# Moving the preparation of the down weights one pass earlier in a linear-attention and gated-FFN kernel

## The chip, the cores and the metric

The kernel runs on one core of a Trainium2 chip. The metric is the device time of one execution in microseconds. The core has a matrix engine (TensorE, in the profile PE, with its weight loads as PEld), VectorE (DVE), ScalarE (ACT), GpSimd (POOL) and SyncE (SP), which here issues every DMA. Each engine works through its own instructions in program order and waits on semaphores for the others.

## The reference

```python
def _A_ref(x, wqkv, wo):                       # linear attention, 32 heads of 32
    qkv = reshape(x @ wqkv)
    phi = lambda t: where(t > 0, t + 1, exp(t)) + 1e-6
    pq, pk = phi(q), phi(k)
    kv = einsum("bhsd,bhse->bhde", pk, v);  z = einsum("bhsd->bhd", pk)
    o = einsum("bhqd,bhde->bhqe", pq, kv) / (einsum("bhqd,bhd->bhq", pq, z)[..., None] + 1e-6)
    return reshape(o) @ wo

def _B_ref(x, w_gate, w_up, w_down):           # gated FFN, no nonlinearity
    return ((x @ w_gate) * (x @ w_up)) @ w_down

x = x + _A_ref(_layernorm(x), A_wqkv, A_wo)
x = x + _B_ref(_layernorm(x), B_w_gate, B_w_up, B_w_down)
x = x + _A_ref(_layernorm(x), A_wqkv, A_wo)    # the same weights a second time
x = x + _B_ref(_layernorm(x), B_w_gate, B_w_up, B_w_down)
```

x has 2048 rows of 1024 in bfloat16, and the FFN is 3584 wide (`F`).

## The kernel before, in words

The rows x stay on chip in the tile `X`. Layer li = 0 and 2 is the attention (`layer_A`), li = 1 and 3 the FFN (`layer_B`). Work buffers come from three queues that are filled and emptied in program order: 16 `slots` of [128 x 4096] bfloat16, 13 `temps` of [128 x 512] float32 and the 8 PSUM `banks`. Whoever takes a buffer waits until its last user has left it. The order of instructions on every engine is the order in which the program writes them: plans of the form `at(step, f, args)` hang side work onto the steps of a matmul loop.

**Attention.** A first phase computes k and v and their sums. The query phase then runs 44 steps (`NQ + OLAG`). In step i it issues the denominator of item i - 4 (`den_step`, `LAG` 4: a matmul, two ACT functions, and L490, a product on DVE of two tiles in SBUF), the query product of item i (`q_step`, 8 matmuls, then in `phi` one ACT function and the DVE operations L193 and L194), and the output product of item i - 12 (`out_step`, 8 matmuls, L498, and the DVE addition L500 into `X`). An item is one of 8 column blocks of one of 4 row groups; the output product of a group needs all eight columns of it. `ahead_of` adds the layer norm and the transposes (through DMA) for the next FFN from step 18, the first two loads of FFN weights at 22 and 28, their casts on ACT from 25, and their sums on DVE at 35 and 41, with `t_sums`, sums of the rows, between.

**FFN.** `ffn_pass` is run four times (q = 0 to 3): two passes of 1024 rows in each of the two FFN layers. A pass has 14 `quad`s, each 256 columns of gate and of up. A quad computes its two products as seven block products instead of eight (Strassen's scheme in the form of Winograd): 14 groups of 4 matmuls (L622), whose partial sums ACT copies out (L627, L668) and DVE adds (L630) and multiplies (L633). Since block sums need a fixed scale, the weights are cast to float16 with a power of two that follows from their size, `scw`.

- In pass q = 0 each quad also casts the weights of quad j + 2 (`W.cast`, L294, four casts of 128x1024 on ACT), forms their sums (`W.sums`, L309, four on DVE) and writes both to a scratch in memory, `wcache` (`W.store`). The later passes read them from there.
- The down product of pass q = 0 is `down_plain`: four blocks of 28 x 4 matmuls (L778) with bfloat16 weights. Beside it, ACT squares the down weights (L746) to find their size, and `scale_begin(1)`, `scale_end(1)` turn this into a scale: a sum on DVE, a transpose on TensorE, a few small DVE operations.
- In pass q = 1 the quads 0, 1, 3, 4, 6, 7, 9 (`at_quad`) also prepare the down weights, four rows of blocks at a time: `prep_load`, `prep_cast` (L596, four casts of 128x1024), `prep_sums` (L605, four on DVE) and `prep_store` (four DMAs) into the scratch `dcache`.
- The down product of passes 1 to 3 is `down_seven`: seven block products of 14 x 4 matmuls (L875) that take raw pieces of the down weights, cast on the way (L582), and combined pieces from `dcache`.

In layer 0's first phase `scan` measures the gate and up weights, with squares on ACT (L201) and statistics on DVE (L206). The two lines that order the casts in a quad are

```python
if j + 2 < NQD: W.cast(j + 2, i)
if q == 1 and j in at_quad: prep_cast(at_quad[j], i)
```

and `cast(0)` stands before the copy of L668, `cast(1)` to `cast(3)` behind it.

Of the kernel before, what the change touches and what calls it, by code (L numbers as in the profile page):

```python
# [34 lines left out]
def kernel(  # L35
# [100 lines left out]
    wst = const.tile([P, 32, 6], F32, tag="wst", name="wst")  # L136
    dsq = const.tile([P, 32], F32, tag="dsq", name="dsq")
    bexp = const.tile([P, 3], F32, tag="bexp", name="bexp")
    scw = const.tile([P, 3], F32, tag="scw", name="scw")
    kap = const.tile([P, 2], F32, tag="kap", name="kap")  # L140
    wcache = [dram.tile([P, 2, 4096], F16, tag=f"wc{j}", name=f"wc{j}") for j in range(NQD)]
# [55 lines left out]
    def scan(i):  # L197
# [11 lines left out]
        return square, stats  # L209

    qsum = {}

    def norm_sums(m, q):
        if m == 0:
            nc.vector.tensor_reduce(out=q[:, 0:1], in_=wsq[:, 0:7], axis=AX.X, op=ALU.add)
            nc.vector.tensor_reduce(out=q[:, 1:2], in_=wsq[:, 7:10], axis=AX.X, op=ALU.add)
            mv = small.tile([P, 2], F32, tag="mv", name="mv")
            nc.vector.bn_aggr(out=mv[:], in_=wst[:])
            nc.vector.scalar_tensor_tensor(out=mv[:, 0:1], in0=mv[:, 0:1], scalar=mv[:, 0:1], in1=mv[:, 1:2],
                                           op0=ALU.mult, op1=ALU.add)  # L220
            nc.vector.scalar_tensor_tensor(out=q[:, 1:2], in0=mv[:, 0:1], scalar=float(32 * NB), in1=q[:, 1:2],
                                           op0=ALU.mult, op1=ALU.add)
        else:
            nc.vector.tensor_reduce(out=q[:, 0:1], in_=dsq[:], axis=AX.X, op=ALU.add)

# [13 lines left out]
    def scale_end(m):  # L239
# [17 lines left out]
        nc.vector.tensor_scalar(out=sc, in0=sc, scalar1=WS, scalar2=None, op0=ALU.mult)  # L257
        if m == 0:
            nc.vector.tensor_scalar(out=kap[:, 0:1], in0=bexp[:, 0:1], scalar1=bexp[:, 1:2],
                                    scalar2=(WS * XS) ** -2, op0=ALU.mult, op1=ALU.mult)  # L260
        else:
            nc.vector.tensor_scalar(out=kap[:, 1:2], in0=kap[:, 0:1], scalar1=bexp[:, 2:3],
                                    scalar2=1.0 / (WS * HS), op0=ALU.mult, op1=ALU.mult)

    class Weights:
        def __init__(self, cached):
            self.cached = cached
            self.wt = {}
            self.ws = {}
# [12 lines left out]
        def store(self, j):  # L282
            if not self.cached:
                nc.sync.dma_start(out=wcache[j][:, 0], in_=self.wt[j][:].bitcast(F16))
# [56 lines left out]
    def layer_A(li, ahead):  # L341
# [163 lines left out]

        LAG, OLAG = 4, 12
        NQ = NG * KD
        for i in range(NQ + OLAG):
# [16 lines left out]
            if li == 0 and i == 16:  # L525
                scale_end(0)
            for f, *args in ahead.get(i, []):
                f(*args)
# [12 lines left out]
    def ffn_pass(li, p, W):  # L541
# [8 lines left out]
        final = li == 3 and p == 1  # L550

        def load_wd(n, i):
            s = slots.get()
            nc.sync.dma_start(out=s[:, 0:WPC * NB].rearrange("p (k n) -> p k n", n=NB),
                              in_=wd_v[:, i * WPC:(i + 1) * WPC, n * NB:(n + 1) * NB])
            wd.append(s)

# [26 lines left out]

        def first_wd(i):
            if q == 0:
                load_wd(0, i)
            else:
                load_piece()

        at_quad = {0: 0, 1: 1, 3: 2, 4: 3, 6: 4, 7: 5, 9: 6}
# [21 lines left out]
        def quad(j):  # L613
            a, b, c = ([banks.get() for _ in range(2)] for _ in range(3))
            if j % 2 == 0:
                hs.append(slots.get())
            hv = (v3 if q == 0 else h3)(hs[j // 2], 2 * G)
            u1, u2, u3 = {}, {}, {}
# [13 lines left out]
            def mul(r, g, x, y):  # L632
                nc.vector.scalar_tensor_tensor(out=hv[:, 2 * (j % 2) + r, g * G:(g + 1) * G], in0=x[:],  # L633
                                               scalar=kap[:, 0:1] if q == 0 else HS, in1=y[:],
                                               op0=ALU.mult, op1=ALU.mult)

            def cast(i):
                if j + 2 < NQD:
                    W.cast(j + 2, i)
                if q == 1 and j in at_quad:  # L640
                    prep_cast(at_quad[j], i)
                if q > 0 and j == NQD - 1 and i < 2:
                    cast_piece(0, (i,))
# [44 lines left out]
        for j in range(NQD):  # L688
            if j + 2 < NQD:
                W.load(j + 2)  # L690
            elif j == NQD - 2:
                first_wd(0)
            else:
                first_wd(1)
                first_wd(2)
            if q == 1 and j - 1 in at_quad:
                prep_store(at_quad[j - 1])
            if q == 1 and j in load_at:
                prep_load(load_at[j])
            quad(j)  # L700
            if j + 2 < NQD:
                W.sums(j + 2)
            if q == 1 and j in at_quad:
                prep_sums(at_quad[j])
# [26 lines left out]
        nl = (li, 1) if p == 0 else (li + 1, 0)  # L731
        W2 = Weights(True)
        if q == 0:
            down_plain(li, p, hs, wd, load_wd, at, run, finish, xrow, nl, W2)
        else:
            down_seven(li, p, hs, wd, load_piece, cast_piece, ORDER, at, run, finish, xrow, nl, W2, load_a, final)
        return W2

    def down_plain(li, p, hs, wd, load_wd, at, run, finish, xrow, nl, W2):
        load_wd(0, 3)  # L740

        def square(i):
            for r in range(4):
                w = WPC * NB // 4
                t = temps.get()
                nc.scalar.activation(out=t[:].bitcast(BF16)[:, 0:w], in_=wd[i][:, r * w:(r + 1) * w],  # L746
                                     func=ACT.Square, accum_out=dsq[:, 4 * i + r:4 * i + r + 1])
                temps.put(t)

        for u in range(2 * TPG):  # L750
            t = nl[1] * 2 * TPG + u
            at(1 + 3 * u, ln_stats, nl[0], t)
            at(2 + 3 * u, ln_norm, nl[0], t)
            at(3 + 3 * u, tr_tile, nl[0], t)
        for i in range(3):
            at(6 + 7 * i, load_wd, 1, i)
        for i in range(4):
            at(3 + 7 * i, square, i)
        for i in range(4):
            at(KF + 24 + 5 * i, square, 4 + i)  # L760
        at(KF + 21, load_wd, 1, 3)
        for i in range(4):
            at(2 * KF + 10 + 5 * i, t_sums, li, 1, i)
        at(3 * KF + 8, W2.load, 0)
        at(3 * KF + 17, W2.load, 1)
        at(3 * KF + 21, prep_load, 0)
        at(3 * KF + 25, prep_load, 1)
        at(3 * KF, scale_begin, 1)
        at(3 * KF + 6, scale_end, 1)

        for blk in range(4):
            n, g = divmod(blk, 2)
            bs = [banks.get() for _ in range(TPG)]
            for f in range(KF):
                s = wd[n * NPC + f // WPC]
                for tl in range(TPG):
                    t0 = g * G + tl * P
                    nc.tensor.matmul(out=bs[tl][:], lhsT=v3(hs[f // 4], 2 * G)[:, f % 4, t0:t0 + P],  # L778
                                     rhs=s[:, (f % WPC) * NB:(f % WPC + 1) * NB],
                                     start=(f == 0), stop=(f == KF - 1), skip_group_check=True)  # L780
                if g == 1:
                    if f % WPC == WPC - 1:
                        slots.put(s)
                    if n == 1 and f % 4 == 3:
                        slots.put(hs[f // 4])
                run(blk * KF + f)
            for tl in range(TPG):
                _, o, _ = xrow(g, tl, n)
                nc.vector.tensor_tensor(out=o, in0=o, in1=bs[tl][:], op=ALU.add)
                banks.put(bs[tl])  # L790
                finish(g, tl, n)

    def down_seven(li, p, hs, wd, load_piece, cast_piece, ORDER, at, run, finish, xrow, nl, W2, load_a, final):
        sg = [slots.get(), slots.get()]
# [36 lines left out]
        if not final:  # L831
            if p == 0:
                for i in range(4):
                    at(60 + 4 * i, t_sums, li, 1, i)
                at(75, W2.load, 0)
                at(89, W2.load, 1)
            else:
# [8 lines left out]
        def read(o, g, tl, n, src, keep=None):  # L846
            _, x, _ = xrow(g, tl, n)
            nc.vector.scalar_tensor_tensor(out=o, in0=src, scalar=kap[:, 1:2], in1=x if keep is None else keep,
                                           op0=ALU.mult, op1=ALU.add)
# [51 lines left out]
    def ahead_of(li, W):  # L901
# [16 lines left out]
        at(41, W.sums, 1)  # L918
        at(42, W.store, 0)
        at(43, W.store, 1)  # L920
        return plan
# [6 lines left out]
    for li in (0, 2):  # L928
        W = Weights(li > 0)
        layer_A(li, ahead_of(li + 1, W))  # L930
# [31 lines left out]
```

## Time and profile before

| what | value |
|---|---|
| median of 3 runs | 1526.24 us (1525.51 to 1526.77) |
| the profiled execution, its own time | 1525.0 us |
| span of the profiled execution | 1523.2 us |
| DVE busy | 950.8 us (62%) |
| ACT busy | 678.6 us (45%) |
| DMA | 249.44 MB, mean 164 GB/s |

The span runs from the first to the last instruction in the trace; the time of the same execution is 1.8 us longer. A group in the profile reads: line, engine, operation, output <- inputs, sizes, count, busy microseconds, mean nanoseconds of one, idle time of the engine before it, and what ended that. Matmuls are pipelined: a busy share of TensorE near 100% says that it always had one in hand. In a timeline the bracket behind a line gives the engine's idle time before it and the releaser.

### The profile page before, as it was taken

To read this page: it belongs to the slowest core of one execution; us is meant where nothing else is said; L and a number is where in the kernel's file an instruction comes from. 1 tells how busy PE (TensorE), PEld (TensorE's weight loads), DVE (VectorE), ACT (ScalarE), POOL (GpSimd) and SP (SyncE) were. 2 spreads that over 40 slices of the span, in tenths; PEclk is the share of its full clock that TensorE was granted. 3 is DMA by queue.
4 is the path that set the end of the run, shared out by engine and by line. 5 is a ranking of instruction groups with operands and counts; after the bars stand their busy time and mean duration, and the time that the engine had idled before them with its cause. 6 is when DMAs were issued, how large, how long until landed. Compare 5 with 4: busy or idle time off the path is not lost.

```text
span 1523.2 us, 18375 instructions
## 1 busy us (share of the span) xinstructions
PE 1511.1 (99%) x7211; PEld 694.2 (46%) x7211; DVE 950.8 (62%) x1595; ACT 678.6 (45%) x1067; POOL 1.7 (0%) x18
## 2 busy tenths in 40 slices
PE   7999999999999999999999999999999999999999
PEld 3454444444444444444444444444444444444444
DVE  6567888777762376657355557865555864555552
ACT  4678665666562255532223355533334222333320
POOL 0000000000000000000000000000000000000000
PEclk9999999999999999999999999999999999999999
DMA  7693045888670776737513300464333578333523
GB/s 242 160 304 97 5 93 179 275 250 267 220 176 28 277 281 240 266 141 207 197 21 83 91 0 8 145 215 158 139 111 128 155 259 336 123 138 139 188 78 128
DMA packets 185287, 249.44 MB, mean 164 GB/s; under 512 B 68209, under 2 KB 162161, under 8 KB 170865
## 3 DMA queue, kind: packets, MB, share of 16 engines
q1 hardware_dynamic: 185200, 248.28, 50.6%
q8 instruction: 56, 0.92, 0.2%
q14 instruction: 31, 0.25, 0.1%
HBM read 191.63 MB, written 40.89 MB: 153 GB/s over the span
## 4 chain that ended last, share of the span: by engine, by line
PE 96%; DVE 2%; ACT 1%; DMA 0%; issue 0%; ACTq 0%
PE b L622 44%; PE b L875 17%; PE b L351 12%; PE b L469 7%; PE b L498 7%; PE b L778 6%; PE b L483 1%; PE b L368 1%; ACT s L201 1%; DVE wst L206 1%; PE b L451 0%; DVE st L157 0%; DVE s L194 0%; DVE f L193 0%; DMA X<-in_A_x_dram 0%; DVE xn L169 0%
## 5 line engine op out<-in xcount | busy, mean ns | idle before, releaser
L622 PE MATMUL b<-s,s 128*128 128x512 f16 x3136 | 677.5, 379 | 0.0
L622 PEld LDWEIGHTS <-s 128*128 128x128 f16 x3136 | 306.8, 98 | 370.0
L627 ACT COPY f<-b 128x512 f32<-128x512 f32 x336 | 196.9, 586 | 409.4 <-PE b L622 409.4
L630 DVE TENSOR_TENSOR f<-f,b 128x512 f32<-128x512 f32 x336 | 229.8, 685 | 237.2 <-ACT f L627 223.2
L875 PE MATMUL b<-s,s 128*128 128x512 f16 x1176 | 254.3, 379 | 0.0
L351 PE MATMUL b<-s,s 128*128 128x512 bf16 x1024 | 224.5, 381 | 2.1 <-DMA s<-in_A_wqkv_dram 1.8
L875 PEld LDWEIGHTS <-s 128*128 128x128 f16 x1176 | 115.1, 98 | 138.7
L351 PEld LDWEIGHTS <-s 128*128 128x128 bf16 x1024 | 100.2, 98 | 122.1 <-issue 2.8
L192 ACT ACTIVATE f<-b 128x512 f32<-128x512 f32 x128 | 75.7, 596 | 109.8 <-PE b L351 85.6
L469 PE MATMUL b<-s,s 128*128 128x512 bf16 x512 | 120.3, 379 | 0.0
L498 PE MATMUL b<-s,s 128*128 128x512 bf16 x512 | 118.5, 379 | 0.0
L582 ACT ACTIVATE s<-s,scw 128x1792 f16<-128x1792 bf16 x36 | 62.3, 1782 | 80.9 <-DMA s<-in_B_w_down_dram 80.9
L778 PE MATMUL b<-s,s 128*128 128x512 bf16 x448 | 96.9, 379 | 0.0
L193 DVE TENSOR_SCALAR f<-f 128x512 f32<-128x512 f32 x128 | 53.8, 420 | 68.5 <-ACT f L192 67.9
L633 DVE SCALAR_TENSOR_TENSOR s<-f,f 128x512 f16<-128x512 f32 x126 | 87.2, 692 | 8.4 <-DMA dc<-s 4.1
L157 DVE BATCH_NORM_STATS2 st<-X 128x6 f32<-128x512 bf16 x128 | 81.8, 681 | 3.6 <-DMA X<-in_A_x_dram 3.6
L498 PEld LDWEIGHTS <-s 128*128 128x128 bf16 x512 | 50.0, 98 | 60.6 <-DVE s L490 0.4
L469 PEld LDWEIGHTS <-s 128*128 128x128 bf16 x512 | 50.0, 98 | 59.7 <-issue 0.3
L778 PEld LDWEIGHTS <-s 128*128 128x128 bf16 x448 | 43.8, 98 | 52.7
L485 ACT ACTIVATE f<-b,eps 128x512 f32<-128x512 f32 x64 | 44.2, 691 | 45.4 <-PE b L483 45.4
L169 DVE TENSOR_SCALAR xn<-X,mv,rstd 128x1024 bf16<-128x1024 bf16 (+1 forms) x64 | 34.8, 544 | 47.2 <-ACT rstd L167 46.7
L294 ACT ACTIVATE s<-s,scw 128x1024 f16<-128x1024 bf16 x56 | 61.4, 1142 | 0.9 <-DMA s<-in_B_w_gate_dram 0.9
(81 smaller groups left out, 852.8 us busy)
## 6 DMA issues: line engine op xcount, KB each, us to landing
s<-wc SPq DMA_DIRECT2D x84, 1024.0 KB, 6.5
wc<-s SPq DMA_DIRECT2D x28, 1024.0 KB, 5.1
s<-in_B_w_down_dram SPq DMA_DIRECT2D x26, 896.0 KB, 5.1
s<-dc SPq DMA_DIRECT2D x24, 896.0 KB, 5.8
s<-in_A_wqkv_dram SPq DMA_DIRECT2D x12, 1024.0 KB, 7.7
s<-in_B_w_up_dram SPq DMA_DIRECT2D x7, 1024.0 KB, 7.9
s<-in_B_w_gate_dram SPq DMA_DIRECT2D x7, 1024.0 KB, 10.2
s<-in_B_w_gate_dram SPq DMA_DIRECT2D x14, 512.0 KB, 6.7
```

Of the source, the lines that this page charges most:

```text
L157: nc.vector.bn_stats(out=st[:, c, :], in_=X[:, t, c * FMAX:(c + 1) * FMAX])
L192: nc.scalar.activation(out=m[:], in_=b[:], func=ACT.Exp)
L351: nc.tensor.matmul(out=b[:], lhsT=xnT[:, k, tl * P:(tl + 1) * P], rhs=w[:, k, :], start=(k == 0), stop=(k == KD - 1))
L469: nc.tensor.matmul(out=b[:], lhsT=w[:, k, j * P:(j + 1) * P], rhs=xnT[:, k, :], start=(k == 0), stop=(k == KD - 1))
L498: nc.tensor.matmul(out=b[:], lhsT=v3(pqs[g], G)[:, c, tl * P:(tl + 1) * P], rhs=v3(M[n], NB)[:, c, :], start=(c == 0), stop=(c == KD - 1))
L582: nc.scalar.activation(out=v.bitcast(F16)[:, r * w:(r + 1) * w], in_=v[:, r * w:(r + 1) * w], func=ACT.Copy, scale=scw[:, 2:3])
L622: nc.tensor.matmul(out=o[m][:], lhsT=W.get(j, m, st[i - 1], k), rhs=mv[i - 1][:, k, :], start=start and k == 0, stop=stop and k == KH - 1, ...
L627: nc.scalar.copy(out=d[m][:], in_=o[m][:])
L630: nc.vector.tensor_tensor(out=d[m][:], in0=d[m][:], in1=o[m][:], op=ALU.add)
L633: nc.vector.scalar_tensor_tensor(out=hv[:, 2 * (j % 2) + r, g * G:(g + 1) * G], in0=x[:], scalar=kap[:, 0:1] if q == 0 else HS, in1=y[:], ...
L778: nc.tensor.matmul(out=bs[tl][:], lhsT=v3(hs[f // 4], 2 * G)[:, f % 4, t0:t0 + P], rhs=s[:, (f % WPC) * NB:(f % WPC + 1) * NB], start=(f = ...
L875: nc.tensor.matmul(out=bank[(key, tl)][:], lhsT=lhs(i, j, tl), rhs=h3(wd[2 * pi + j // WPC], NB)[:, j % WPC, :], start=(j == 0 and i in (1 ...
```

## The change

The size of the down weights is now measured in the query phase of layer 0 instead of in the first down pass. A new function `load_rows` loads them in seven parts (r = 0 to 6). For r below 4 GpSimd squares a part and adds it to a sum, for r = 4 and 5 ACT squares it with a running sum, and for r = 6 DVE takes the largest absolute value, which stands for that part. The scale follows at steps 35 and 38.

The first pass (q = 0) then prepares the combined down weights (`prep_*`) and uses `down_seven`; `down_plain`, `load_wd` and the separate scale `kap[:, 0:1]` are gone. The `wcache` writes move to pass q = 1, which therefore loads, casts and combines the gate and up weights once more from their source; passes 2 and 3 read the scratch as before.

```diff
+    def load_rows(r):
+        s = slots.get()
+        nc.sync.dma_start(out=v3(s, D), in_=wd_v[:, 4 * r:4 * r + 4, :])
+
+        def use():
+            if r < 4:
+                if r == 0:
+                    wsum.append(slots.get())
+                    nc.gpsimd.tensor_tensor(out=wsum[0][:], in0=s[:], in1=s[:], op=ALU.mult)
+                else:
+                    nc.gpsimd.tensor_tensor(out=s[:], in0=s[:], in1=s[:], op=ALU.mult)
+                    nc.gpsimd.tensor_tensor(out=wsum[0][:], in0=wsum[0][:], in1=s[:], op=ALU.add)
+            elif r < 6:
+                nc.scalar.activation(out=s[:], in_=s[:], func=ACT.Square, accum_out=dsq[:, r - 4:r - 3])
+            else:
+                nc.vector.tensor_reduce(out=dsq[:, 2:3], in_=s[:], axis=AX.X, op=ALU.max,
+                                        apply_absolute_value=True)
+            slots.put(s)
+        return use
...
-            nc.vector.tensor_reduce(out=q[:, 0:1], in_=dsq[:], axis=AX.X, op=ALU.add)
+            nc.vector.tensor_reduce(out=q[:, 0:1], in_=wsum[0][:], axis=AX.X, op=ALU.add)
+            slots.put(wsum.pop())
+            nc.vector.tensor_tensor(out=dsq[:, 2:3], in0=dsq[:, 2:3], in1=dsq[:, 2:3], op=ALU.mult)
+            nc.vector.tensor_reduce(out=q[:, 1:2], in_=dsq[:], axis=AX.X, op=ALU.add)
+            nc.vector.tensor_tensor(out=q[:, 0:1], in0=q[:, 0:1], in1=q[:, 1:2], op=ALU.add)
...
     class Weights:
-        def __init__(self, cached):
-            self.cached = cached
+        def __init__(self, q):
+            self.cached = q > 1
+            self.keep = q == 1
...
         def store(self, j):
-            if not self.cached:
+            if self.keep:
...
+            if li == 0:
+                for r, (t0, t1) in enumerate(((1, 5), (7, 11), (11, 14), (16, 19), (19, 22), (23, 26), (27, 30))):
+                    if i == t0:
+                        todo.append(load_rows(r))
+                    if i == t1:
+                        todo.pop(0)()
+            if li == 0 and i == 35:
+                scale_begin(1)
+            if li == 0 and i == 38:
+                scale_end(1)
...
-                if q == 1 and j in at_quad:
+                if q == 0 and j in at_quad:
                     prep_cast(at_quad[j], i)
...
-            if q == 1 and j - 1 in at_quad:
+            if q == 0 and j - 1 in at_quad:
                 prep_store(at_quad[j - 1])
-            if q == 1 and j in load_at:
+            if q == 0 and j in load_at:
                 prep_load(load_at[j])
             quad(j)
             if j + 2 < NQD:
                 W.sums(j + 2)
-            if q == 1 and j in at_quad:
+            if q == 0 and j in at_quad:
                 prep_sums(at_quad[j])
...
-        W2 = Weights(True)
-        if q == 0:
-            down_plain(li, p, hs, wd, load_wd, at, run, finish, xrow, nl, W2)
-        else:
-            down_seven(li, p, hs, wd, load_piece, cast_piece, ORDER, at, run, finish, xrow, nl, W2, load_a, final)
+        W2 = Weights(q + 1)
+        down_seven(q, li, p, hs, wd, load_piece, cast_piece, ORDER, at, run, finish, xrow, nl, W2, load_a, final)
...
-                at(75, W2.load, 0)
-                at(89, W2.load, 1)
+                if q == 0:
+                    at(74, W2.load, 0)
+                    at(77, W2.load, 1)
+                    for i in range(4):
+                        at(82 + i, W2.cast, 0, i)
+                        at(86 + i, W2.cast, 1, i)
+                    at(88, W2.sums, 0)
+                    at(92, W2.sums, 1)
+                    at(95, W2.store, 0)
+                    at(97, W2.store, 1)
+                else:
+                    at(75, W2.load, 0)
+                    at(89, W2.load, 1)
...
-        at(42, W.store, 0)
-        at(43, W.store, 1)
+        if li == 1:
+            at(39, prep_load, 0)
+            at(41, prep_load, 1)
```

## The prediction, made before the changed kernel had run

> **What bounds the kernel now.** I read the head of the page first.
>
> ```profile
> PE 1511.1 (99%) x7211; PEld 694.2 (46%) x7211; DVE 950.8 (62%) x1595; ACT 678.6 (45%) x1067; POOL 1.7 (0%) x18
> ...
> PEclk9999999999999999999999999999999999999999
> ```
>
> TensorE is busy from end to end at the full granted clock, so the time is a count of matmuls, and any work that makes TensorE wait is lost at once. POOL has done nothing but its 18 start-up instructions. Next, the chain of work in order of time (start us, us, what):
>
> ```profile
> 237.20 15.65 PE b L498 x72
> 252.85 169.21 PE b L622 x784
> 422.06 78.56 PE b L778 x364
> 500.68 18.13 PE b L778 x84
> 518.81 169.21 PE b L622 x784
> 688.03 84.61 PE b L875 x392
> ```
>
> These are the tail of the first query phase, the quads of pass 1, its plain down product (L778, 448 matmuls, 96.7 us), the quads of pass 2, and its seven-product down pass (392 matmuls, 84.6 us). None has a gap. A quad is 169.21 / 14 = 12.09 us: 14 products of 4 matmuls, 0.863 us a product. Then windows of one quad each (columns: PE, PEld, DVE, ACT, POOL busy, clock, DMA share, GB/s): one of pass 1, with weight casts and sums, and one of pass 2, with down preparation.
>
> ```profile
> 301.19:313.28 12.09, 12.09 (x58) 5.48 (x56) 9.42 (x15) 8.28 (x12) 0.00 (x0) 1.00 0.84 262
> ...
> 567.15:579.24 12.09, 12.09 (x58) 5.49 (x56) 9.38 (x15) 8.28 (x12) 0.00 (x0) 1.00 0.81 260
> ```
>
> Each alone leaves ACT 3.8 us and DVE 2.7 us of the quad. How the casts lie in that time shows in ACT's timeline of the first quads of pass 2:
>
> ```profile
> 526.29 1.15 ACT L596 ACTIVATE s<-s,scw 128x1024 f16<-128x1024 bf16 x1
> 527.54 0.59 ACT L668 COPY f<-b 128x512 f32<-128x512 f32 x1
> 528.02 3.23 ACT L596 ACTIVATE s<-s,scw 128x1024 f16<-128x1024 bf16 x3
> 531.86 0.59 ACT L627 COPY f<-b 128x512 f32<-128x512 f32 x1 [0.61 <-PE b L622]
> ```
>
> One cast comes before the copy of L668, three after it in a bunch, and then ACT is idle 0.61 us before the first copy of the next quad. That copy empties the bank into which product 6, the fourth of the quad, accumulates.
>
> **The down pass.** 448 matmuls become 392: 56 x 0.2158 us = **-12.1 us**. The 32 squares of L746 go, but they were beside the matmuls. The six-piece casts, block sums and reads that come instead are those of the pass at 688.03, which runs without a gap. New in it are two weight loads, eight casts (8 x 1.04 us) and eight sums (8 x 0.73 us) in its last 17 steps; ACT is idle there, and what follows needs them only at its first and second quad. Cost 0. If that cover fails, it is about 3 us.
>
> **Pass 2.** It takes over pass 1's weight loads, casts, sums and scratch writes, and loses its own preparation. It becomes what pass 1 was, with 9.4 us of DVE and 8.3 of ACT in 12.09 and a DMA share of 0.84, which ran without a gap. Cost 0.
>
> **Pass 1.** It keeps casts and sums and gains the preparation, in seven quads (0, 1, 3, 4, 6, 7, 9). In ACT's program order every weight cast is now followed by a preparation cast. Two casts stand before L668's copy, which moves from 527.54 to 528.37, and six after it: 528.85 + 6 x 1.04 = 535.1. The next quad's first copy then ends at 535.7 instead of 532.45. Product 6 starts at 530.90 + 3 x 0.863 = 533.5, so TensorE waits 2.2 us. The wait puts both engines back in step, so it comes again at each such quad: 7 x 2.25 = **+15.8 us**. DVE has two sets of sums, 6.7 + 2 x 2.9 = 12.5 us, in a quad that now lasts 14.3 us; it ends about when the delayed quad first needs it. The queue of SP has the four scratch writes of a row between two weight loads, but carries 1 MB of writes where it had 2, so I give it nothing (against it: one weight load, in quad 6, waits for the landing of such writes, 1 to 2 us).
>
> **The end of the query phase.** Two reductions of 128x4096 are put on DVE, at step 30 and, as the head of the scale chain, at step 35. The nearest row is L247: 293 ns for 128 elements and 417 for 256, so 0.97 ns each, and 4.1 us for 4096. DVE has idle 0.45 + 0.23 + 0.98 us between 231 and 240, so the first leaves it 2.4 us late. It ended the add of step 35 at 240.8; with 2.4, 4.1 and about 1.0 for the small operations the scale chain is ready at 248.3. At step 38 TensorE has to transpose its result. In the old timing it gets there at 237.2 + 4 x 1.73 = 244.1, and waits 4.2 us; with the transpose and a bank that DVE empties late (product 5 of quad 0, 0.8 us) this is **+5.3 us**. Its bounds are 0, if the reduction runs at twice that rate, and 10. The squares on ACT (2 x 3.6 us, the row of L201) delay a den chain that has 3 us of room: 0, at most 2. SP has seven loads of 1 MB ahead of its transposes and first weight loads. Two of those now also wait until POOL has left the slot, long before they are due unless POOL is late.
>
> **POOL beside DVE.** Seven operations of 128x4096, four products and three sums, go to POOL from about 135 us, when the first rows have landed. Nothing in the trace shows POOL with two inputs. The nearest rows, from the groups of instructions (xcount | busy, mean ns):
>
> ```profile
> masks.py:199 POOL TENSOR_SCALAR_AFFINE_SELECT ident<-ident 128x128 bf16<-128x128 bf16 x1 | 0.3, 294 | 0.1
> ...
> L122 POOL MEMSET eps<- 128x1 f32 x1 | 0.1, 104 | 0.1
> ...
> L193 DVE TENSOR_SCALAR f<-f 128x512 f32<-128x512 f32 x128 | 53.8, 420 | 68.5 <-ACT f L192 67.9
> ...
> L194 DVE SCALAR_TENSOR_TENSOR f<-b,f 128x512 bf16<-128x512 f32 x64 | 44.3, 692 | 2.2
> ...
> L490 DVE TENSOR_TENSOR s<-f,f 128x512 bf16<-128x512 bf16 x64 | 43.3, 676 | 17.0 <-ACT f L487 16.9
> ```
>
> One input costs (294 - 104) / 127 = 1.5 ns an element, 6.2 us for 4096; two inputs lie between that and its double, 12.3. I take the middle, 9.2: seven are 64 us (43 to 86). POOL itself is waited for by nobody until the sum is read at step 35. The question is what DVE does meanwhile: between 138 and 161 us it has no idle time at all. L193 takes 420 ns where L194 takes 692 for as many elements, so it moves more than one element at a time, and L490 reads two tensors of SBUF; whatever second path they use was never asked for by another engine in this trace. From below the cost is 0, or below it no gain: nothing is taken from DVE. From above, DVE stands still for each POOL operation at the next L193 or L490. There are two of these in a query step of 2.37 us, so half a step gets through per POOL operation, 7 x 1.2 = 8 us of progress; TensorE can run on for some three steps, 7 us. Lost: 64 - 8 - 7 = **+49 us** (28 to 71). I take the upper case, since an operation that moves two streams needs two paths, and POOL needs one for its own two inputs.
>
> The Trainium skill, "SBUF — State Buffer", Who interferes with whom, says that GpSimd and VectorE share a pair of SBUF ports, held for a whole instruction, and that a VectorE operation with two SBUF inputs or in a two-port mode waits until the other has finished. By that rule the sum is the upper one; without it, the cost of POOL is zero. "GPSIMD Engine Reference", section 3.1, gives 2.6 cycles an element for two inputs, which I estimate at 8.9 us an operation at its 1.2 GHz, 62 us for seven. No run shown here can confirm either.
>
> **Sum.** -12.1 + 15.8 + 5.3 + 49 = +58 us. On the profiled execution (span 1523.2, its time 1525.0) this is a time of 1583; the median of the runs, 1526.24, is 1.2 above that execution, so **1584**.
>
> **Rivals.**
> 1. POOL disturbs nobody: the same sum without 49, +9 us, **1535**. For it: no row shows the two engines in each other's way.
> 2. DVE's two-stream operations only run at half speed meanwhile. A step has 0.35 + 0.60 us of them, so it takes 3.25 us where TensorE's takes 2.37: in 64 us DVE gets through 19.7 steps, 46.7 us of TensorE's work, and 17 are lost, 15 after the room it has: **1550**.
> 3. Faster: the seven products' 12.1 us come in full, **1514**, because the casts do not reach TensorE, and POOL and the reductions are hidden. It turns on the price of a cast behind a cast: six must fit in the 4.0 us from 528.85 to the latest start of the next copy, 532.9, so 0.67 us each. The row says 1.04, three times over, and POOL must be harmless as well.
>
> **How the numbers follow.** Forecast (POOL holds DVE) 0.55; rival 1: 0.22; rival 2: 0.15; rival 3: 0.08. The forecast's own range is 28 to 71 for POOL, 1563 to 1606. To hold 8 in 10 it must reach down to rival 1: 1531, with the reductions priced near 1, up to 1602. This kernel's runs can tell about 0.2%, 3 us, from no change. Rival 3 is the faster case, of which some lands near zero when only part of the casts is hidden: faster 0.07, same 0.03, slower 0.90.
>
> **What would show it.** In the profile after: a chain piece of 392 matmuls, 84.6 us, for the first down pass; after each of the seven double quads about 2.2 us in which TensorE waits for ACT's copy; DVE idle behind POOL between 135 and 220 us, with L193 or L490 stretched to several us; POOL operations of 6 to 12 us; reductions of 4 us, and TensorE waiting for DVE at step 38. L193 at 420 ns beside a running POOL makes the forecast wrong and rival 1 right; copies that meet product 6 in time make rival 3 right.

## The result

The changed kernel takes 1588.49 us (median of 6 runs, 1587.33 to 1590.43), beside 1526.32 for the kernel before on the same chip: 1.0408 times as long, with a 95% interval of 1.0394 to 1.0421. The forecast was 1584, in a range of 1531 to 1602. The profiled execution has a span of 1586.4 us, 63.2 more than before.

The head of its page, first the busy times, then the slices of the span (each 39.7 us):

```profile
PE 1513.5 (95%) x7155; PEld 691.5 (44%) x7155; DVE 1064.3 (67%) x1695; ACT 732.1 (46%) x1075; POOL 54.1 (3%) x25
...
PE   7996489888899999999999999999999999999999
...
POOL 0006510000000000000000000000000000000000
PEclk9997789999999999999999999999999999999999
```

TensorE has 56 matmuls less, and holes in the slices in which POOL works; its granted clock (the row PEclk) falls there too. The later slices are as full as before. Line numbers have moved: quads are now L645, their copies L650 and L691, weight casts L318, preparation casts L619, down products L852. The chain of work in order of time (start us, us, what) from the last double quad on:

```profile
451.68 45.92 PE b L645 x212
497.60 84.61 PE b L852 x392
582.21 169.21 PE b L645 x784
751.42 84.61 PE b L852 x392
```

The first down pass is 84.61 us instead of 96.7, and pass 2 is 169.21 with the weight casts, sums and scratch writes it took over. So everything that was lost was lost before 497.60. POOL's timeline shows where it began (the idle time of POOL and its releaser in brackets):

```profile
134.17 7.01 POOL L219 TENSOR_TENSOR s<-s 128x4096 bf16<-128x4096 bf16 x1 [131.68 <-ACT s L201]
141.15 7.19 POOL L221 TENSOR_TENSOR s<-s 128x4096 bf16<-128x4096 bf16 x1
148.42 7.97 POOL L222 TENSOR_TENSOR s<-s,s 128x4096 bf16<-128x4096 bf16 x1
156.36 7.00 POOL L221 TENSOR_TENSOR s<-s 128x4096 bf16<-128x4096 bf16 x1
163.44 7.97 POOL L222 TENSOR_TENSOR s<-s,s 128x4096 bf16<-128x4096 bf16 x1
188.23 7.15 POOL L221 TENSOR_TENSOR s<-s 128x4096 bf16<-128x4096 bf16 x1 [16.83 <-DMA s<-in_B_w_down_dram]
195.46 8.23 POOL L222 TENSOR_TENSOR s<-s,s 128x4096 bf16<-128x4096 bf16 x1
```

Five operations back to back, a pause until the slot of part 3 was free and loaded, and two more: 52.5 us. DVE's timeline of the same time:

```profile
134.48 6.99 DVE L193 TENSOR_SCALAR f<-f 128x512 f32<-128x512 f32 x1 [6.14 <-ACT f L192]
141.50 0.69 DVE L194 SCALAR_TENSOR_TENSOR f<-b,f 128x512 bf16<-128x512 f32 x1
...
143.90 27.99 DVE L456 TENSOR_SCALAR s<-mask,z 128x128 bf16<-128x128 f32 x8
171.80 0.41 DVE L193 TENSOR_SCALAR f<-f 128x512 f32<-128x512 f32 x1
...
189.81 6.12 DVE L514 TENSOR_TENSOR s<-f,f 128x512 bf16<-128x512 bf16 x1
195.85 8.13 DVE L193 TENSOR_SCALAR f<-f 128x512 f32<-128x512 f32 x1
```

An L193 that had taken 0.42 us ends at 141.5, 0.3 us behind POOL's operation. L194, which reads one input from PSUM and one from SBUF, takes its 0.69 while the next one runs. Eight scalings of the mask (L456), 1.64 us together before, take 28.0 us beside four operations of POOL and end just behind the fifth (171.4). When POOL pauses everything has its old duration; when it starts again, L514 and L193 wait once more. TensorE waits for these results:

```profile
142.52 1.81 PE L464 MATMUL b<-ident,s 128*128 128x128 bf16 x8 [4.05 <-DVE s L454]
148.48 0.61 PE L507 MATMUL b<-f,s 128*128 128x512 bf16 x1 [4.16 <-DVE s L456]
...
173.00 0.59 PE L507 MATMUL b<-f,s 128*128 128x512 bf16 x1 [19.64 <-DVE f L194]
...
204.75 3.57 PE L493 MATMUL b<-s,s 128*128 128x512 bf16 x8 [11.94 <-DVE f L194]
```

The first output product, at 159.60 before, starts at 208.32, 48.7 us late; eight steps on it is 49.0 (192.73 to 241.76), and 0.4 of that was there before POOL began.

The query phase then loses some more at its end, and the pass its seven waits. TensorE's timeline:

```profile
290.29 0.39 PE L522 MATMUL b<-s,s 128*128 128x512 bf16 x1 [0.69 <-DVE s L514]
292.26 0.39 PE L522 MATMUL b<-s,s 128*128 128x512 bf16 x1 [1.58 <-DVE s L514]
294.54 5.32 PE L522 MATMUL b<-s,s 128*128 128x512 bf16 x17 [1.89 <-DVE s L514]
300.43 0.23 PE L270 MATMUL b<-ident,f 128*128 128x128 bf16 x1 [0.57 <-DVE f L260]
300.49 8.80 PE L522 MATMUL b<-s,s 128*128 128x512 bf16 x40
309.12 1.89 PE L645 MATMUL b<-s,s 128*128 128x512 f16 x8
311.94 13.11 PE L645 MATMUL b<-s,s 128*128 128x512 f16 x60 [0.93 <-DMA s<-in_B_w_up_dram]
327.22 13.93 PE L645 MATMUL b<-s,s 128*128 128x512 f16 x56 [2.17 <-ACT f L650]
...
369.83 12.25 PE L645 MATMUL b<-s,s 128*128 128x512 f16 x56 [2.17 <-ACT f L650]
```

The quads begin at 309.12 instead of 252.69, 56.4 late: 49.0 from POOL's time and the start, 7.4 from here. A double quad is one with both sets of casts. The seven quads of pass 1 behind a double quad each begin product 6 with 2.17 us of wait for ACT's copy; with the time that the stream of matmuls needs to fill again a wait costs 2.33 (343.33 to 369.83, less 112 x 0.2158). Two quads with 56 matmuls stand in the last lines: one takes 13.93 us, the other 12.25. That difference is the clock, to which the experiments come back.

The account of the span: +48.6 POOL, +0.4 the start, +7.4 the end of the query phase, +19.3 pass 1 (7 x 2.33, 1.1 for a late weight load, 1.7 for the clock, and 0.2 that I can't place), -12.1 the down pass, together 63.6 against 63.2 measured.

### The profile page after: what moved, and what is told of

It is laid out like the page before. It is cut to its first block, busy times and chain, and to the rows that moved or that the text cites. A ratio compares the mean times of both kernels' runs of the same rounds, so it can differ in the third digit from the quotient of the medians.

```text
span 1586.4 us, 18438 instructions
## 1 busy us (share of the span) xinstructions
PE 1513.5 (95%) x7155; PEld 691.5 (44%) x7155; DVE 1064.3 (67%) x1695; ACT 732.1 (46%) x1075; POOL 54.1 (3%) x25
## 4 chain that ended last, share of the span: by engine, by line
PE 84%; DVE 8%; ACT 7%; DMA 1%; issue 1%; SPq 0%; ACTq 0%
PE b L645 39%; PE b L852 21%; PE b L375 12%; PE b L493 5%; PE b L522 5%; ACT s L318 2%; DVE s L456 2%; ACT s L619 2%; DVE f L193 1%; ACT s L201 1%; DVE s L514 1%; PE b L392 1%; DVE wst L206 1%; PE b L507 1%; DMA s<-in_A_wqkv_dram 0%
## 5 line engine op out<-in xcount | busy, mean ns | idle before, releaser
L645 PE MATMUL b<-s,s 128*128 128x512 f16 x3136 | 680.5, 380 | 16.1 <-ACT f L650 15.2
L645 PEld LDWEIGHTS <-s 128*128 128x128 f16 x3136 | 307.2, 98 | 388.8 <-issue 20.6
L650 ACT COPY f<-b 128x512 f32<-128x512 f32 x336 | 195.8, 585 | 347.4 <-PE b L645 347.4
L852 PE MATMUL b<-s,s 128*128 128x512 f16 x1568 | 339.1, 379 | 0.0
L852 PEld LDWEIGHTS <-s 128*128 128x128 f16 x1568 | 153.4, 98 | 185.0
L375 PE MATMUL b<-s,s 128*128 128x512 bf16 x1024 | 225.1, 381 | 1.8 <-DMA s<-in_A_wqkv_dram 1.5
L375 PEld LDWEIGHTS <-s 128*128 128x128 bf16 x1024 | 100.3, 98 | 122.0 <-issue 3.1
L493 PE MATMUL b<-s,s 128*128 128x512 bf16 x512 | 125.4, 391 | 12.4 <-DVE f L194 12.4
L318 ACT ACTIVATE s<-s,scw 128x1024 f16<-128x1024 bf16 x112 | 124.2, 1144 | 3.5 <-DMA s<-in_B_w_gate_dram 2.6
L611 ACT ACTIVATE s<-s,scw 128x1792 f16<-128x1792 bf16 x48 | 83.0, 1782 | 92.4 <-DMA s<-in_B_w_down_dram 57.3
L522 PE MATMUL b<-s,s 128*128 128x512 bf16 x512 | 120.8, 383 | 4.4 <-DVE s L514 4.2
L656 DVE SCALAR_TENSOR_TENSOR s<-f,f 128x512 f16<-128x512 f32 x168 | 116.3, 692 | 5.8
L193 DVE TENSOR_SCALAR f<-f 128x512 f32<-128x512 f32 x128 | 68.1, 532 | 69.1 <-ACT f L192 68.5
L493 PEld LDWEIGHTS <-s 128*128 128x128 bf16 x512 | 51.0, 100 | 95.7 <-issue 38.7
L522 PEld LDWEIGHTS <-s 128*128 128x128 bf16 x512 | 50.5, 99 | 67.2 <-DVE s L514 5.2
L825 DVE SCALAR_TENSOR_TENSOR X<-b,kap,f 128x512 bf16<-128x512 f32 x48 | 32.7, 743 | 60.6 <-PE b L852 60.6
L514 DVE TENSOR_TENSOR s<-f,f 128x512 bf16<-128x512 bf16 x64 | 48.8, 763 | 19.6 <-ACT f L511 19.1
```

The costliest lines, as they stand in the source:

```text
L193: nc.vector.tensor_scalar(out=m[:], in0=m[:], scalar1=1.0, scalar2=1e-6, op0=ALU.min, op1=ALU.add)
L318: nc.scalar.activation(out=h, in_=v, func=ACT.Copy, scale=scw[:, m:m + 1])
L375: nc.tensor.matmul(out=b[:], lhsT=xnT[:, k, tl * P:(tl + 1) * P], rhs=w[:, k, :], start=(k == 0), stop=(k == KD - 1))
L493: nc.tensor.matmul(out=b[:], lhsT=w[:, k, j * P:(j + 1) * P], rhs=xnT[:, k, :], start=(k == 0), stop=(k == KD - 1))
L522: nc.tensor.matmul(out=b[:], lhsT=v3(pqs[g], G)[:, c, tl * P:(tl + 1) * P], rhs=v3(M[n], NB)[:, c, :], start=(c == 0), stop=(c == KD - 1))
L611: nc.scalar.activation(out=v.bitcast(F16)[:, r * w:(r + 1) * w], in_=v[:, r * w:(r + 1) * w], func=ACT.Copy, scale=scw[:, 2:3])
```

## The experiments

Each run starts from the changed kernel. My theory was the sum on record: GpSimd holds a path that some VectorE operations need, bunched casts delay a copy, and two reductions delay the scale. Its rivals were the SP queue with its new loads, the mere amount of ACT and VectorE work, and reductions that are hidden.

**no_pool.** GpSimd's operations are left out; the slot of part 0 goes to the reduction as loaded (a maximum in place of a sum), the others are freed.

```diff
-                    nc.gpsimd.tensor_tensor(out=wsum[0][:], in0=s[:], in1=s[:], op=ALU.mult)
-                else:
-                    nc.gpsimd.tensor_tensor(out=s[:], in0=s[:], in1=s[:], op=ALU.mult)
-                    nc.gpsimd.tensor_tensor(out=wsum[0][:], in0=wsum[0][:], in1=s[:], op=ALU.add)
+                    wsum.append(s)
+                    return
...
-            nc.vector.tensor_reduce(out=q[:, 0:1], in_=wsum[0][:], axis=AX.X, op=ALU.add)
+            nc.vector.tensor_reduce(out=q[:, 0:1], in_=wsum[0][:], axis=AX.X, op=ALU.max)
```

> GpSimd's seven operations are left out, so parts 0 to 3 of the down weights are not squared (the sum at step 35 reads part 0 as loaded, with a maximum); all loads, slots, the ACT squares and both DVE reductions stay. Theory (GpSimd holds the path that VectorE's two-stream operations need): the 48.6 us by which the query phase is late at its step 12 go, L193 and L514 fall back to 420 and 676 ns, and the time is about 1540 us. Rival (the seven loads and the transposes and weight loads that queue behind them on SP): they all stay, so at least 40 of the 49 us stay and the time is above 1575.

Measured: 1543.29 us (1538.85 to 1550.13), and L193 is back at a mean of 421 ns. The loads on SP all remained, so they are not the cause; the rival is out. Here they no longer wait until POOL has left a slot, but against a queue held up in that way speak the lines above, where TensorE waits for VectorE and not for a transfer. The runs spread by 11 us, which I had not expected; it is taken up below.

**pool_writes_only.** GpSimd works about as long, on the same tiles and in the same order, but only writes.

```diff
-                    nc.gpsimd.tensor_tensor(out=s[:], in0=s[:], in1=s[:], op=ALU.mult)
-                    nc.gpsimd.tensor_tensor(out=wsum[0][:], in0=wsum[0][:], in1=s[:], op=ALU.add)
+                    for _ in range(2):
+                        nc.gpsimd.memset(s[:], 2.0 ** -18)
+                for _ in range(2):
+                    nc.gpsimd.memset(wsum[0][:], 2.0 ** -18)
```

> Each GpSimd operation becomes two memsets of the same tile (14 in all, some 3.4 us each by the slope of the small memsets), so GpSimd works about as long but reads nothing; the measured size is a constant. If only GpSimd's reads are in VectorE's way: no loss, about 1540 us. If a VectorE operation in its two-port mode (L193, the L456 of the mask) waits for any GpSimd operation, but L514, which only needs a second read, does not: L193 stretched to 3 us and more, L514 at 0.68, and since one such operation passes per memset, some 20 to 35 us lost, 1560 to 1575 us.

Measured: 1567.95 us (1566.47 to 1569.33), 1.0275 times the kernel before (1.026 to 1.029), and 27.6 us above no_pool, lowest to lowest. The fourteen memsets took 51 us. DVE's timeline in that run, while POOL was in its memsets of 158.40 and 185.26:

```profile
163.10 0.68 DVE L515 TENSOR_TENSOR s<-f,f 128x512 bf16<-128x512 bf16 x1
163.70 2.49 DVE L193 TENSOR_SCALAR f<-f 128x512 f32<-128x512 f32 x1
...
186.84 0.68 DVE L515 TENSOR_TENSOR s<-f,f 128x512 bf16<-128x512 bf16 x1
187.44 1.89 DVE L193 TENSOR_SCALAR f<-f 128x512 f32<-128x512 f32 x1
```

The product of two SBUF tensors (here L515) keeps its 0.68 us beside a memset, and L193, which takes 0.42 us when POOL is idle, waits. That is how the Trainium skill has it ("SBUF — State Buffer", Who interferes with whom): a VectorE operation in a two-port mode waits for any GpSimd operation, one with two SBUF inputs only for a GpSimd operation that reads. This run and the changed kernel agree with both halves (L514 took 6.12 us beside a POOL operation that reads), and a held operation waits for the end of the GpSimd instruction that is running. The memsets are half as long as the operations that they replace and hold up fewer kinds of instruction; which of the two makes the loss smaller than POOL's 48.6 is not separated.

**casts_spread.** The preparation casts get other places in the quad, and nothing else changes: one each behind the second copies of products 1 and 6, one with the first weight cast, one behind the bunch.

```diff
+            def early(i):
+                if q == 0 and j in at_quad:
+                    prep_cast(at_quad[j], i)
...
             copy(u1, a, 1)
+            early(1)
...
             copy(u2, a, 1)
+            early(2)
...
-                if q == 0 and j in at_quad:
-                    prep_cast(at_quad[j], i)
+                if i in (0, 3):
+                    early(i)
```

> The order of the 28 preparation casts within the quads is changed, nothing else: two of the four go into the two gaps of 1.14 us between early copies, one stays before the copy of L691, one behind the bunch. Theory (the bunch of six delays the first copy of the next quad): the seven waits of 2.17 us and the 1.7 us of slow clock behind the first go, 1588.5 - 17 = about 1571 us. Rival (ACT has 12 us of work in a quad of 12.09, or VectorE 12.5, whatever the order): a wait of a similar size stays, and the time is within 5 us of 1588.

Measured: 1571.66 us (1570.71 to 1573.87). The amount of ACT work is unchanged (732.3 us busy, 732.1 in the changed kernel), and no wait of TensorE's matmuls for ACT's copies is left in the list of waits. The order was the cause, not the sum of ACT's or DVE's work.

**best_try.** The casts spread, and only parts 4 and 5 measured.

```diff
-                for r, (t0, t1) in enumerate(((1, 5), (7, 11), (11, 14), (16, 19), (19, 22), (23, 26), (27, 30))):
+                for r, (t0, t1) in ((4, (19, 22)), (5, (23, 26))):
...
```

The branches for the other parts, both long reductions and the sum `wsum` go with them; the casts are ordered as in casts_spread.

> Casts spread as in the run before, and only parts 4 and 5 of the down weights are measured (two squares on ACT): no GpSimd work, no long VectorE reductions, five loads fewer; the scale is set from two of seven parts. Theory: of the sum only -12.1 us is left, with up to 3 us for the first quad: 1514 to 1518 us. Rival (pass 1 is bound by the sums of ACT and VectorE work, or the down pass's new casts reach TensorE): 1522 or more.

Measured: 1516.59 us (1515.36 to 1516.80), 0.9937 times the kernel before (0.9922 to 0.9952). It beats both kernels, the one before by 0.6%. Of the 12.1 us of the down pass 8.5 arrive in the span: the first quad starts 1.85 us later than before (1.02 of it is there at the start of the query phase), and pass 1 takes 170.99 us in place of 169.21, about 0.25 a double quad. The scale cancels in the result, so its measure only has to keep float16 in range; here a sample of the weights does that, which is less of a guard than the original's full sum. A version that measures all seven parts at this time was not tried.

**casts_bunched.** best_try with the change's own order of casts.

> The kernel of best_try with the casts in the change's own order again (measured from parts 4 and 5 alone, no GpSimd, no long reductions). Theory of the waits: seven of 2.17 us, 1516.6 + 15.2 = 1531.8 us when the clock holds. Theory of the clock (a wait of 2.2 us makes the granted clock drop for some 4 us in some quads and not in others, 1.7 us each): single runs spread between 1532 and 1544 us, and the profile's own time fits the number of quads of which the 56 matmuls take 13.9 us instead of 12.25. Rival (the clock is not touched by waits this short): all runs within 3 us of each other, near 1532.

Measured: 1533.28 us (six runs: 1531.48, 1532.48, 1533.22, 1533.33, 1540.05, 1540.30). The lowest is 16.1 above the lowest of best_try. The seven waits, less the 0.25 us that a double quad of best_try loses too, are 7 x 2.08 = 14.6 of it. The remaining 1.5 can be the start, which differs by up to 1 us between profiles, or one drop of the clock: the mean granted clock was 0.999 in this run and 1.000 in best_try's. The profiled execution is the one of 1540.05; its TensorE timeline:

```profile
272.12 13.93 PE L629 MATMUL b<-s,s 128*128 128x512 f16 x56 [2.17 <-ACT f L634]
288.22 26.02 PE L629 MATMUL b<-s,s 128*128 128x512 f16 x112 [2.17 <-ACT f L634]
316.42 13.93 PE L629 MATMUL b<-s,s 128*128 128x512 f16 x56 [2.17 <-ACT f L634]
332.52 26.02 PE L629 MATMUL b<-s,s 128*128 128x512 f16 x112 [2.17 <-ACT f L634]
360.72 13.93 PE L629 MATMUL b<-s,s 128*128 128x512 f16 x56 [2.17 <-ACT f L634]
376.82 24.33 PE L629 MATMUL b<-s,s 128*128 128x512 f16 x112 [2.17 <-ACT f L634]
403.33 45.92 PE L629 MATMUL b<-s,s 128*128 128x512 f16 x212 [2.17 <-ACT f L634]
```

Seven equal waits, and behind five of them the next matmuls take 1.69 us more (13.93 for 12.25, 26.02 for 24.33). Five times 1.69 is 8.5 us, and this run is 8.6 above the lowest. In the profile of no_pool all seven are slow, 11.8 us, and its execution is 11.3 us above its lowest.

**casts_half.** As casts_bunched, but one preparation cast stands in an early gap, so that five are in the bunch.

> As casts_bunched, but one of the four preparation casts lies in an early gap, so five stand in the bunch instead of six. The waits should fall by one cast, from 2.17 to 1.13 us: 7 x 1.13 = 7.9 us over best_try, 1524.5 us. If short waits do not make the clock drop, single runs agree within 3 us; if every wait can, the spread is as in casts_bunched.

Measured: 1523.39 us (1522.74 to 1524.24 in 11 runs). Two lines of its TensorE timeline:

```profile
269.52 12.25 PE L629 MATMUL b<-s,s 128*128 128x512 f16 x56 [1.13 <-ACT f L634]
282.90 24.33 PE L629 MATMUL b<-s,s 128*128 128x512 f16 x112 [1.13 <-ACT f L634]
```

The wait is shorter by the 1.04 us of one cast, at each of the seven quads, and none of them has slow matmuls behind it. All 11 runs lie within 1.5 us.

**no_pool_spread.** no_pool with the casts of casts_spread.

> no_pool with the casts spread: what is left beside the -12.1 us is the end of the query phase with its two VectorE reductions of 4.4 us, the squares and the seven loads. Theory: 4.4 us of waits of TensorE for VectorE, 0.5 for a bank, and 1 to 3 us of slow clock behind them, 1516.6 + 6 to 8 = about 1523 us. Rival (the reductions are hidden, and the waits seen in the other runs come from the late start): 1518 or less.

Measured: 1523.27 us (1522.82 to 1524.44 in 10 runs), 6.7 above best_try. TensorE's timeline at the end of its query phase:

```profile
242.13 0.39 PE L519 MATMUL b<-s,s 128*128 128x512 bf16 x1 [0.69 <-DVE s L511]
244.10 0.39 PE L519 MATMUL b<-s,s 128*128 128x512 bf16 x1 [1.58 <-DVE s L511]
246.37 5.30 PE L519 MATMUL b<-s,s 128*128 128x512 bf16 x17 [1.88 <-DVE s L511]
252.26 0.23 PE L267 MATMUL b<-ident,f 128*128 128x128 bf16 x1 [0.59 <-DVE f L257]
```

These are the same waits as in the changed kernel, without POOL before them, so the late start did not make them, and the rival is out. The pair with casts_spread differs by POOL alone: 1571.66 - 1523.27 = 48.4 us, the price of the seven operations. (The two ran on different chips, on which the kernel before took 1525.93 and 1525.73 us.)

## Why the prediction was right, point by point

- *The down pass, -12.1.* 84.61 us for 392 matmuls; the new loads, casts and sums in its tail cost nothing.
- *Pass 2, 0.* 169.21 us, as said.
- *Pass 1, +15.8.* The seven waits are 2.17 us where 2.25 was worked out from the row of one cast; the place (product 6) and the return at each double quad are as described. Refill and one drop of the clock make it 18.0, and a weight load in quad 0, which I had seen as a risk in quad 6, adds 1.1.
- *The reductions, +5.3.* They take 4.41 us each instead of 4.1, and the waits add up to 4.95, 0.22 for a bank among them. The path was another. Most of the wait came earlier than I said: not at the transpose of step 38 (0.57), behind the second reduction, but at the first output product of the last row group (0.69, 1.58 and 1.89), which needs the L514 of steps 33 to 35. These are late through the first reduction (L226, 278.52 to 282.93): the layer norm's sums stand on DVE behind it, ACT waits 5.32 us for them in L165 and 2.30 in the next one, and the denominators that L514 multiplies with stand on ACT behind L165. In best_try, without the long reductions, 0.71 us of these waits is left. That the waits add up to a size so near the sum's is luck. The refill behind each and the clock, 0.54 to 0.61 between 294 and 298 us, bring it to 7.4.
- *POOL, +49.* 48.4 to 48.6 measured. The mechanism is as described, but the number comes out of two wrong terms that cancel, by luck. The operations took 7.0 to 8.2 us, not 9.2, so 52.5 us and not 64. In return DVE and TensorE got through less than the 15 us I allowed: the first five operations met the eight mask scalings, short operations that are no part of a step and of which only two got through per GpSimd operation, and the lead of TensorE was spent at once, because the transposes of step 3 and the denominators of steps 4 and 5 already wait for DVE's first results. The Trainium skill's rate of 2.6 cycles an element ("GPSIMD Engine Reference", section 3.1), 8.9 us by my estimate, was also above the trace.
- *The rivals.* "POOL disturbs nobody" fails on L193 at 7 us; "half speed" fails because L193 stands still and does not slow down; "faster" fails on the price of a cast, 1.04 us, and returns as best_try once the casts are spread, POOL is out and the measure is short.

## What to carry to other kernels

An engine that is idle in the profile is not free: look for what it shares with the engine beside it, and price its operation by the instructions that must wait for the whole of it, the shortest ones too. When an engine has room in a loop body, ask at which place of its queue the room lies; four casts more cost 2.3 us in a bunch before a copy that frees a bank, and about 0.25 in the gaps. Before work is brought forward, count where it lands, since the tail of a phase (one reduction ahead of sums that the last denominators wait behind, another ahead of a transpose that TensorE itself must do) has no cover.

## What the runs showed of the hardware that was not expected

A short wait can cost nearly twice its length. Behind some of the waits of 2.17 us the granted clock of TensorE was 0.50 for 3.41 us (read in windows of 0.1 us; over 4 us that averages 0.57), and behind others of the same execution it stayed at 1.00. Each drop cost 1.7 us. Four profiles have seven such waits each, and of these none (pool_writes_only), one (the changed kernel), five (casts_bunched) and seven (no_pool) had a drop behind them. The number of drops accounts for the distances between profiled and lowest executions in casts_bunched and no_pool, if the lowest had none.

Which waits are hit can be read from the same profiles. In casts_bunched the drops begin at 272.41, 289.48, 316.79, 333.85 and 361.16 us, and the later four lie 5, 13, 18 and 26 times 3.413 us behind the first. The seven of no_pool lie on such a grid too. So in these executions the clock changed only at marks 3.413 us apart, wherever the kernel's waits fell. Continue each profile's grid over all its waits (for pool_writes_only from a drop at 183.57), and the 28 part: the 13 with a drop behind them have at least 2.08 us of their idle time between two neighbouring marks, and the drop begins at the second; the 15 others have at most 2.01. These are estimates from the windows, good to some 0.02 us. A wait of 1.13 us is too short for that, and in casts_half none of the seven was followed by slow matmuls.

The Trainium skill ("TensorE: Matmul & The Clock Gate", Part 1) describes half rate after an idle window of about 3.4 us that runs freely, not from the kernel's start. The half rate, the length and the free run are what these traces show; that about 2.1 us of idle time in a window suffices is less than the page says.
